# Attention and gated expert layer on one core: the masks built on DVE from index patterns instead of by GpSimd selections

## The chip, the cores and the metric

One Trainium2 chip, one core. The metric is the device time of one execution in microseconds, from the device's own clock; lower is better. Engines are named as in the profile: PE (TensorE's matrix multiplies), PEld (its weight loads), DVE (VectorE), ACT (ScalarE), POOL (GpSimd) and SP (the queue that issues the DMAs). Each engine takes its instructions strictly in program order and waits at the first one that isn't ready.

## What is computed

```python
B, H, S, D = 4, 8, 768, 64; block, window = 32, 16
k_sum = k.reshape(B, H, 24, 32, D).max(axis=3)
v_sum = v.reshape(B, H, 24, 32, D).mean(axis=3)
mask_l = np.abs(pos[:, None] - pos[None, :]) < window
scores_l = np.where(mask_l, scale * q @ k.T, -1e9)
scores_s = scale * q @ k_sum.T + np.log(32)
a = softmax(np.concatenate([scores_l, scores_s], -1))
attn = a @ np.concatenate([v, v_sum], axis=2)
x = attn.transpose(0, 2, 1, 3).reshape(B * S, H * D)      # 3072 x 512
out = ((x @ w_a) * (x @ w_b)) @ w_out                     # w: 512 x 1536, 512 x 1536, 1536 x 512
```

Each query sees the 31 keys nearest to it and 24 block summaries; then every row of 512 values goes through the gated layer. All is float32 at the edges; the matrix products run in a rounded 32-bit form with a high and a low part for each operand.

## The kernel before

**Tiles and stages.** The attention works on 128 queries at a time, in two halves of 64 (QT). A half needs a window of 96 keys (WIN) and the 24 summaries, so 120 score columns (COLS). The expert layer works on chunks of two or three such tiles; the list of (chunk, slice of the 1536 inner columns) is called items. The first two chunks (FILL = 2) go through eight of the twelve slices together as one wide item (PAIR), while the weights arrive from HBM and are converted (`convert`, lines 386 to 427: ACT L405, DVE L408 and L416, ACT L421, POOL L424, once for each of 36 weight parts). All later chunks use the converted weights. The head is what happens until the first items run: K tiles are loaded (L342) and turned on PE (L441), DVE takes block maxima (L508), ACT puts the keys into place (L500, L501), Q is turned and scaled (L938), masks are added on PE (L650), scores are made on PE (L663).

**The masks.** A tile `mask` of 128 partitions (query), 3 kinds (first tile of a sequence, inner tile, last tile) and 128 columns holds -1e9 where a key isn't seen, 0 where it is, and log 32 over the summaries. It is made on POOL (lines 214 to 237 and 322): one memset, then for each kind a row of `affine_select` (L229, 21 in all) and two small memsets (L234). Kinds 0 and 1 are made first, then POOL builds `pairs` (L241, L243), casts the identity (L317), splits the first two kinds into a high and a low part `maskr` (L318, L319), and makes kind 2 last. The first four tiles of attention add `maskr` on PE (L650); all later ones add `mask` on DVE (L692). DVE begins with three memsets (L252 twice for the value tiles `vbuf`, L253).

**The order of work.** Nothing is ordered by a compiler: every operation is handed to `Work.add` with an engine, a rank, an expected duration and the data that it reads and writes. `emit` then plays a simple clock: each engine takes the ready operation of the lowest rank, and the instructions are emitted in the order of that play. Two things steer it: `ORDER` (line 24), lists of operation numbers that fix the beginning of each engine's order, and `Work.free` (line 325), the time at which each engine is free when the play starts. When an engine's list is used up, the planner chooses by rank and by its own clock; past 70 us of that clock it adds a margin (SLACK) to what comes from another engine.

Of the kernel before, what the change touches and what calls it, by code (L numbers as in the profile page):

```python
# [10 lines left out]
F32R = mybir.dt.float32r  # L11
# [4 lines left out]
ALU = mybir.AluOpType  # L16
AX = mybir.AxisListType
LOG32 = 3.4657359027997265
NEG = -1.0e9
# [10 lines left out]
    ],  # L30
    "ACT": [
# [8 lines left out]
    ],  # L40
    "DVE": [
# [8 lines left out]
    ],  # L50
    "POOL": [
# [3 lines left out]
    ],  # L55
# [6 lines left out]
    ],  # L62
}

# [79 lines left out]
def attention_moe(  # L144
# [10 lines left out]
    nc = tc.nc  # L155
    B, H, S, D = q.shape
    P = 128
# [4 lines left out]
    QT = 64  # L162
    BLK = 32
    NS = S // BLK
    WIN = 96
    COLS = WIN + NS
    CH = 256
    G = CH // P
    WIDE = 3
# [17 lines left out]
    def sb(shape, name, dtype=F32):  # L187
        return const.tile(shape, dtype, tag=name, name=name)

    ident = sb([P, P], "ident")  # L190
    make_identity(nc, ident)

# [19 lines left out]
    kper = kT[:, :, : KC - 32].rearrange("p c (i x) -> p c i x", x=PER)  # L212

    mask = sb([P, 3, P], "mask")
    nc.gpsimd.memset(mask, 0.0)

    def mask_kind(i):
        for e in range(2):
            es = slice(e * QT, (e + 1) * QT)

            for c0, n, w in ((0, WIN, 0),) if e == 0 else ((0, 32, 0), (32 + NS, 64, 32)):
                sl = mask[es, i, c0 : c0 + n]
                bounds = [(1, w - 1, -1), (-1, 31 - w, 1)]
                if i == 0 and e == 0:
                    bounds.append((1, w - 16, 0))
                if i == 2 and e == 1:
                    bounds.append((-1, 79 - w, 0))
                for step, base, per_query in bounds:
                    nc.gpsimd.affine_select(  # L229
                        out=sl, in_=sl, compare_op=ALU.is_ge, fill=NEG, base=base,  # L230
                        pattern=[[step, n]], channel_multiplier=per_query,
                    )
            k0 = WIN if e == 0 else 32
            nc.gpsimd.memset(mask[es, i, k0 : k0 + NS], LOG32)  # L234

    mask_kind(0)
    mask_kind(1)


    pairs = sb([P, 96], "pairs")  # L240
    nc.gpsimd.memset(pairs, 1.0 / BLK)  # L241
    for base, sign in ((32, 1), (-31, -1)):
        nc.gpsimd.affine_select(  # L243
            out=pairs, in_=pairs, compare_op=ALU.is_ge, fill=0.0, base=base,
            pattern=[[-2 * sign, 96]], channel_multiplier=sign,
# [3 lines left out]
    pbuf = sb([P, 2, NP, P], "pt")  # L249
    vbuf = [sb([P, H, D], f"vw{e}") for e in range(2)]  # L250
    for e in range(2):
        nc.vector.memset(vbuf[e], 0.0)  # L252
    nc.vector.memset(sbuf[:, :, :, COLS:], 0.0)  # L253
    xt = sb([P, 9, NP, P], "x", F32R)
    last = xt[:, 0].rearrange("p c x -> p (c x)")
    gt, gg = sb([P, 2 * CH], "g"), sb([P, 2 * WIDE * P], "gh", F32R)
    ght, glt = gg[:, : WIDE * P], gg[:, WIDE * P :]
    gs = [gt[:, i * CH : (i + 1) * CH] for i in range(2)]
    ghs, gls = [ght[:, :CH], last[:, :CH]], [glt[:, :CH], last[:, CH:]]
# [1 line left out]
    half = sb([P, S // P, 8], "half")  # L261
# [46 lines left out]
    def area(i):  # L308
# [5 lines left out]
    maskr = [  # L314
        x[:, n : n + 2 * P].rearrange("p (i x) -> p i x", x=P) for n in (P, 3 * P)
    ]
    nc.gpsimd.tensor_copy(out=identr, in_=ident)  # L317
    nc.gpsimd.tensor_copy(out=maskr[0], in_=mask[:, :2, :])  # L318
    nc.gpsimd.tensor_tensor(  # L319
        out=maskr[1], in0=mask[:, :2, :], in1=maskr[0].bitcast(F32), op=ALU.subtract  # L320
    )
    mask_kind(2)


    work = Work({"POOL": 10.9, "DVE": 2.3, "ACT": 2.3, "PE": 3.0, "SP": 0.8})

    def pe(rank, takes, reads, writes, fn):
        work.add("PE", rank, takes, 0.25, reads, writes, fn)
# [949 lines left out]
```

## Time and profile before

| what | value |
|---|---|
| median of 3 runs | 654.04 us (653.34 to 654.15) |
| span of the profiled execution, first to last instruction | 652.4 us |
| own time of the profiled execution | not listed apart from the runs; its span is 1.6 us below their median |
| TensorE's mean granted clock | 0.997 of full speed |
| busy: PE, PEld, DVE, ACT, POOL | 639.0, 591.7, 398.0, 242.6, 155.8 us |

The page counts an engine as busy while one of its compute instructions is under way. A row of a timeline reads: start, duration, engine, source line, operation, output and input, shapes, how many in a row, and in brackets the idle time before it with what ended it. [...] A row of a group reads: line, engine, operation, shapes and count, then total busy us and mean ns of one, then idle time before the group and what ended it.

### The profile page before, as it was taken

The page shows a single profiled execution, that of the slowest core. Times are in us where ns is not written, and L with a number is a line of the kernel's source. Part 1 is how long each engine was busy: PE and PEld are TensorE (multiplying, and loading weights), DVE is VectorE, ACT ScalarE, POOL GpSimd, SP SyncE. Part 2 cuts the span into 40 slices and gives each one's busy share as a digit, 9 for nine tenths or more (in the row PEclk, how much of TensorE's full clock was granted, in tenths as well). Part 3 has the DMA queues.
Part 4 walks back from the last instruction along what each step waited for, and adds up shares of the span by engine and source line. Part 5 has one row for each costly group of instructions (what it writes and reads, how often), then busy time and mean ns, then how long its engine had stood idle before and what let it go on. Part 6 is the DMA issues. An engine that isn't in the chain of part 4 may idle for free.

```text
span 652.4 us, 12782 instructions
## 1 busy us (share of the span) xinstructions
PE 639.0 (98%) x4911; PEld 591.7 (91%) x4911; DVE 398.0 (61%) x866; ACT 242.6 (37%) x694; POOL 155.8 (24%) x238
## 2 busy tenths in 40 slices
PE   7799999999999999999999999999999999999997
PEld 4598888899999999999999999999999999999996
DVE  5877899987887584676676763756766632122212
ACT  4886787324443231422334312343323321121111
POOL 6782667523223222123222100111001100000000
PEclk9899999999999999999999999999999999999999
DMA  9999993552422233513114230142110200010001
GB/s 242 277 284 267 296 240 72 102 125 56 104 63 82 50 72 64 128 39 81 33 34 119 54 56 12 26 102 40 32 25 1 72 1 0 2 49 0 1 1 48
DMA packets 153108, 54.68 MB, mean 84 GB/s; under 512 B 133192, under 2 KB 145736, under 8 KB 153048
## 3 DMA queue, kind: packets, MB, share of 16 engines
q1 hardware_dynamic: 152904, 53.75, 34.0%
q8 instruction: 38, 0.62, 0.4%
q14 instruction: 22, 0.18, 0.1%
q10 hardware_dynamic: 144, 0.13, 0.1%
HBM read 47.12 MB, written 6.29 MB: 82 GB/s over the span
## 4 chain that ended last, share of the span: by engine, by line
PE 90%; DMA 4%; SPq 2%; ACT 1%; POOL 1%; DVE 1%; issue 0%; DVEq 0%; POOLq 0%; ACTq 0%
PE h L1067 55%; PE o L1154 28%; DMA raw<-in_moe_w_b_dram 4%; PE c L663 3%; PE o L816 3%; SPq L342 2%; POOL w L424 1%; PE h L816 0%; ACT S L405 0%; DVE c L408 0%; PE c L816 0%; PE c L1067 0%; POOL space L755 0%; DVE S L416 0%; PE o L768 0%
## 5 line engine op out<-in xcount | busy, mean ns | idle before, releaser
L1067 PE MATMUL h<-x,w 128*128 128x384 f32 (+2 forms) x2100 | 390.5, 320 | 0.1
L1067 PEld LDWEIGHTS h<-x,w 128*128 128x128 f32 x2100 | 334.1, 190 | 9.5 <-DVE x L839 0.7
L1154 PE MATMUL o<-w,gh 128*128 128x512 f32 x731 | 175.2, 382 | 0.0
L1154 PEld LDWEIGHTS o<-w,gh 128*128 128x128 f32 x731 | 134.5, 189 | 18.0 <-issue 2.4
L1135 DVE TENSOR_TENSOR h<-h,g 128x384 f32<-128x384 f32 (+1 forms) x79 | 45.7, 579 | 134.7 <-PE h L1067 134.3
L1137 ACT CAST gh<-h 128x384 fp32r<-128x384 f32 x71 | 34.0, 480 | 220.8 <-DVE h L1135 216.4
L800 DVE STREAM_TRANSPOSE pt<-s 32x256 f32<-32x256 f32 x228 | 99.3, 436 | 11.6 <-POOL s L755 7.9
L755 POOL TENSOR_TENSOR s<-s,nml 128x480 f32<-128x480 f32 x44 | 43.5, 989 | 229.6 <-DVE nml L751 193.6
L1067 PE MATMUL h<-late,w 128*128 128x384 f32 x288 | 94.0, 326 | 0.0
L729 ACT ACTIVATE s<-s,nml 128x120 f32<-128x120 f32 x160 | 61.5, 387 | 35.1 <-DVE nml L700 35.1
L1132 ACT COPY g<-h 128x384 f32<-128x384 f32 (+1 forms) x80 | 39.2, 490 | 55.4 <-PE h L1067 54.5
L1067 PEld LDWEIGHTS h<-late,w 128*128 128x128 f32 x288 | 54.4, 189 | 1.2 <-DVE late L839 0.2
L1140 DVE TENSOR_TENSOR gh<-h,gh 128x384 fp32r<-128x384 f32 x71 | 39.5, 556 | 22.0 <-ACT gh L1137 21.3
L692 DVE SCALAR_TENSOR_TENSOR s<-c,mask 128x480 f32<-128x480 f32 x40 | 26.0, 652 | 26.7 <-PE c L663 26.4
L587 POOL TENSOR_TENSOR S<-S 96x256 f32<-96x256 f32 (+3 forms) x58 | 33.2, 572 | 35.4 <-DMA S<-in_v_dram 32.9
L1154 PE MATMUL o<-w,x 128*128 128x512 f32 (+1 forms) x133 | 32.6, 381 | 0.2 <-DVE x L1108 0.2
L424 POOL TENSOR_TENSOR w<-S,w 128x512 fp32r<-128x512 f32 x24 | 30.4, 1286 | 7.3 <-ACT w L421 6.9
L408 DVE TENSOR_SCALAR c<-raw 128x512 int32<-128x512 uint32 x36 | 28.4, 804 | 5.6 <-DMA raw<-in_moe_w_b_dram 3.0
L729 ACT ACTIVATION_READ_ACCUMULATOR s<-s,nml 128x1 f32 x160 | 30.3, 190 | 0.0
L1154 PEld LDWEIGHTS o<-w,x 128*128 128x128 f32 x133 | 24.4, 189 | 4.2 <-DVE x L1108 0.6
L700 DVE TENSOR_REDUCE nml<-s 128x4 f32<-128x480 f32 x40 | 25.8, 647 | 0.5
L405 ACT ACTIVATE S<-raw 128x512 f32<-128x512 f32 x24 | 20.4, 861 | 4.7 <-DMA raw<-in_moe_w_b_dram 4.3
(138 smaller groups left out, 446.3 us busy)
## 6 DMA issues: line engine op xcount, KB each, us to landing
raw<-in_moe_w_a_dram SPq DMA_DIRECT2D x12, 512.0 KB, 7.7
raw<-in_moe_w_b_dram SPq DMA_DIRECT2D x12, 512.0 KB, 8.6
raw<-in_moe_w_out_dram SPq DMA_DIRECT2D x12, 512.0 KB, 5.7
out_dram<-S SPq DMA_DIRECT2D x23, 256.0 KB, 2.1
S<-in_v_dram SPq DMA_DIRECT2D x24, 192.0 KB, 2.8
kin<-in_k_dram SPq DMA_DIRECT2D x38, 100.0 KB, 2.5
qin<-in_q_dram SPq DMA_DIRECT2D x112, 32.0 KB, 1.9
vw<-in_v_dram SPq DMA_DIRECT2D x17, 192.0 KB, 2.8
```

The costliest lines, as they stand in the source:

```text
L408: dve(rank, 0.66, [raw], [bk], lambda: nc.vector.tensor_scalar(out=z.bitcast(I32), in0=word(0).bitcast(U32), scalar1=2.0**-29, scalar2=7.0 ...
L424: lambda eng=nc.vector if near else nc.gpsimd: eng.tensor_tensor(out=half(1), in0=t, in1=half(0).bitcast(F32), op=ALU.subtract),
L587: lambda: nc.gpsimd.tensor_tensor(out=out, in0=i0, in1=i1, op=ALU.add),
L729: lambda h=h, c=c, more=more: nc.scalar.activation(y[h][:, c, :], x[h][:, c, :], AF.Exp, bias=m[:, 0, h, c : c + 1], scale=1.0, **more,),
L755: lambda h=h, r=r: nc.gpsimd.tensor_tensor(out=y[h], in0=y[h], in1=r[:, :, None].broadcast_to([P, NP, COLS]), op=ALU.mult,),
L800: lambda js=js, qs=qs, rs=rs: nc.vector.transpose(out=pv[js, rs, qs], in_=sv[qs, rs, js]),
L1067: nc.tensor.matmul(ps, w[:, c, part, :], xs[xpart][:, :, c].rearrange("p g (a b) -> p g b a", a=2), start=(i == 0), stop=(i == n - 1),)
L1132: act(CHAIN, 0.13 + W / 1030, ["h0"], gk, lambda: nc.scalar.copy(out=g, in_=pa))
L1135: lambda: nc.vector.tensor_tensor(out=pb, in0=pb, in1=g, op=ALU.mult),
L1137: act(CHAIN, 0.16 + W / 1030, [bk], ghks, lambda: nc.scalar.copy(out=gh, in_=pb))
L1140: lambda: nc.vector.tensor_tensor(out=gl, in0=pb, in1=gh.bitcast(F32), op=ALU.subtract),
L1154: nc.tensor.matmul(b, (gh if first else gl)[:, j * P : (j + 1) * P], y, start=(f == 0 or half is not None) and first and part == 0, stop=( ...
```

## The change

Four edits:

1. POOL no longer makes masks. It writes, by three `iota`, a tile with key offset minus query index minus 16 (partition index with a factor of -1). The tile is `g`, which the items use much later as scratch.
2. DVE squares it, compares with 15.5 squared and multiplies the result by -1e9 for all three kinds at once, then patches with five memsets; the split into `maskr` moves from POOL to DVE too.
3. The two memsets of `vbuf` move from DVE to POOL, behind `pairs`.
4. `Work.free` says 5.0 for POOL (10.9 before) and 5.0 for DVE (2.3 before), and the end of each list in `ORDER` is cut off: 8 operations on PE, 22 on ACT, 24 on DVE, 8 on POOL, 7 on SP. What stays of the lists is unchanged.

```diff
@@ ORDER: the ends of the lists are cut
-        529, 530, 532, 321, 539, 537, 538, 540, 547, 545, 546, 548, 555, 553,
+        529, 530, 532, 321, 539, 537,
...
-        264, 276, 270, 310, 304, 316, 298, 363, 357, 375, 339, 387, 369, 381,
+        264, 276, 270, 310, 304, 316,
...
@@ behind make_identity
+    gt = sb([P, 2 * CH], "g")
+    steps, squares = gt[:, :COLS], gt[:, P : P + COLS]
+    for half, c0, n, w in ((0, 0, COLS, 0), (1, 0, 32 + NS, 0), (1, 32 + NS, 64, 32)):
+        nc.gpsimd.iota(
+            steps[half * QT : (half + 1) * QT, c0 : c0 + n], pattern=[[1, n]], base=w - BLK // 2,
+            channel_multiplier=-1, allow_small_or_imprecise_dtypes=True,
+        )
...
     mask = sb([P, 3, P], "mask")
-    nc.gpsimd.memset(mask, 0.0)
-    def mask_kind(i):
...
-    mask_kind(0)
-    mask_kind(1)
...
     for e in range(2):
-        nc.vector.memset(vbuf[e], 0.0)
+        nc.gpsimd.memset(vbuf[e], 0.0)
...
     nc.gpsimd.tensor_copy(out=identr, in_=ident)
-    nc.gpsimd.tensor_copy(out=maskr[0], in_=mask[:, :2, :])
-    nc.gpsimd.tensor_tensor(
+
+    nc.vector.tensor_tensor(out=squares, in0=steps, in1=steps, op=ALU.mult)
+    nc.vector.tensor_scalar(
+        out=mask[:, :, :COLS], in0=squares[:, None, :].broadcast_to([P, 3, COLS]),
+        scalar1=(BLK / 2 - 0.5) ** 2, scalar2=NEG, op0=ALU.is_gt, op1=ALU.mult,
+    )
+    nc.vector.memset(mask[:, :, COLS:], 0.0)
+    nc.vector.memset(mask[:QT, :, WIN:COLS], LOG32)
+    nc.vector.memset(mask[QT:, :, 32 : 32 + NS], LOG32)
+    nc.vector.memset(mask[:QT, 0, :16], NEG)
+    nc.vector.memset(mask[QT:, 2, COLS - 16 : COLS], NEG)
+    nc.vector.tensor_copy(out=maskr[0], in_=mask[:, :2, :])
+    nc.vector.tensor_tensor(
         out=maskr[1], in0=mask[:, :2, :], in1=maskr[0].bitcast(F32), op=ALU.subtract
     )
-    mask_kind(2)
...
-    work = Work({"POOL": 10.9, "DVE": 2.3, "ACT": 2.3, "PE": 3.0, "SP": 0.8})
+    work = Work({"POOL": 5.0, "DVE": 5.0, "ACT": 2.3, "PE": 3.0, "SP": 0.8})
```

## Rows read from the trace of the kernel before

**Rows 1.** The page: PE's share, and all engines.

```profile
PE 639.0 (98%) x4911; PEld 591.7 (91%) x4911; DVE 398.0 (61%) x866; ACT 242.6 (37%) x694; POOL 155.8 (24%) x238
```

**Rows 2.** Busy time by stretches: head, filling, full load, end.

```profile
0.00:24.00 24.00, 15.65 (x134) 11.14 (x135) 14.10 (x27) 12.60 (x38) 16.14 (x53) 0.95 1.06 263
24.00:60.00 36.00, 35.39 (x402) 31.44 (x401) 27.27 (x57) 28.25 (x65) 23.81 (x24) 0.98 1.01 262
60.00:640.00 580.00, 579.84 (x4334) 541.72 (x4333) 352.99 (x776) 198.66 (x586) 115.89 (x162) 1.00 0.28 66
640.00:652.40 12.40, 8.15 (x47) 7.42 (x45) 3.60 (x7) 3.09 (x6) 0.00 (x0) 1.00 0.17 63
```

**Rows 3.** Timeline of PE, first 20 us.

```profile
4.41 1.09 PE L441 MATMUL h<-ident,space 128*128 128x128 f32 x4 [4.41 <-POOL mask L229]
...
10.29 1.11 PE L441 MATMUL o<-ident,space 128*128 128x128 f32 x4
...
11.90 1.17 PE L650 MATMUL o<-space 128*128 128x512 f32 x4
12.99 1.05 PE L663 MATMUL o<-kT,qT 64*64 64x120 f32 x32
...
19.02 0.65 PE L768 MATMUL o<-ident,s 128*120 128x128 f32 x4 [2.49 <-POOL s L755]
```

**Rows 4.** Timeline of POOL, first 10 us.

```profile
1.09 0.29 POOL masks.py:199 TENSOR_SCALAR_AFFINE_SELECT ident<-ident 128x128 f32<-128x128 f32 x1
...
6.16 0.60 POOL L243 TENSOR_SCALAR_AFFINE_SELECT pairs<-pairs 128x96 f32<-128x96 f32 x2
6.71 0.29 POOL L317 CAST space<-ident 128x128 fp32r<-128x128 f32 x1
...
7.44 0.72 POOL L319 TENSOR_TENSOR space<-mask,space 128x256 fp32r<-128x256 f32 x1
```

**Rows 5.** Groups by line, first 12 us: what is removed or moved.

```profile
L229 POOL TENSOR_SCALAR_AFFINE_SELECT mask<-mask 64x96 f32<-64x96 f32 (+2 forms) x21 | 4.8, 238 | 1.1
...
L252 DVE MEMSET vw<- 128x512 f32 x2 | 1.0, 485 | 1.0 <-PEq L1258 1.0
...
L253 DVE MEMSET s<- 128x64 f32 x1 | 0.1, 112 | 0.0
```

**Rows 6.** Timelines of DVE and ACT in the head, from 5 us.

```profile
5.53 0.69 DVE L508 TENSOR_REDUCE ksum<-h 128x16 f32<-128x512 f32 x1 [3.44 <-PE h L441]
...
7.83 0.43 ACT L500 COPY kT<-c 128x320 f32<-128x320 f32 x1 [0.37 <-PE c L441]
...
11.44 0.69 DVE L508 TENSOR_REDUCE ksum<-o 128x16 f32<-128x512 f32 x1 [0.45 <-PE o L441]
12.17 0.26 DVE L522 COPY kT<-ksum 128x192 f32<-128x192 f32 x1
```

**Rows 7.** Groups by line and shape, whole span: nearest operations to the added ones.

```profile
L1135 DVE TENSOR_TENSOR h<-h,g 128x384 f32<-128x384 f32 x71 | 40.2, 566 | 132.0 <-PE h L1067 131.6
...
L1103 DVE TENSOR_TENSOR h<-h,g 128x256 f32<-128x256 f32 x20 | 8.6, 430 | 10.7 <-ACT g L1100 10.5
...
L570 DVE TENSOR_TENSOR ksum<-half 128x23 f32<-128x23 f32 x12 | 2.6, 218 | 0.0
...
L424 POOL TENSOR_TENSOR w<-S,w 128x512 fp32r<-128x512 f32 x24 | 30.4, 1286 | 7.3 <-ACT w L421 6.9 <-POOL w L424 0.2
...
L1033 POOL MEMSET S<- 128x1024 f32 x1 | 1.0, 964 | 0.0
```

**Rows 8.** Busy time by stretches: the dip of the clock; the stretch newly planned.

```profile
21.00:26.00 5.00, 4.28 (x28) 3.21 (x31) 3.06 (x9) 3.71 (x7) 2.04 (x5) 0.66 1.07 235
81.00:113.00 32.00, 32.00 (x176) 27.73 (x176) 30.41 (x52) 26.37 (x53) 23.35 (x20) 1.00 0.65 155
```

**Rows 9.** Timelines of DVE and PEld where the third chunk begins.

```profile
137.35 0.68 DVE L839 TENSOR_TENSOR x<-c,x 128x512 fp32r<-128x512 f32 x1
...
138.08 2.08 PEld L1067 LDWEIGHTS h<-x,w 128*128 128x128 f32 x18 [0.27 <-DVE x L839]
```

More of the change, by code (lines that the diff above doesn't have):

```diff
@@ L214, in attention_moe @@
     mask = sb([P, 3, P], "mask")
-    nc.gpsimd.memset(mask, 0.0)
-    def mask_kind(i):
[L218 to L234, printed above, removed]
-    mask_kind(0)
-    mask_kind(1)
     pairs = sb([P, 96], "pairs")
@@ L255, in attention_moe @@
     last = xt[:, 0].rearrange("p c x -> p (c x)")
-    gt, gg = sb([P, 2 * CH], "g"), sb([P, 2 * WIDE * P], "gh", F32R)
+    gg = sb([P, 2 * WIDE * P], "gh", F32R)
     ght, glt = gg[:, : WIDE * P], gg[:, WIDE * P :]
```

9 rows, old and new, of the table ORDER are left out of this document.

## The prediction

> **What bounds the kernel now.** I read the page first: PE is busy 98% of the span [rows 1]. Then the busy time by stretches [rows 2], because an average over the span hides where the missing 2% are. From 60 to 640 us PE lacks 0.16 of 580 us, and from 24 to 60 us it lacks 0.61 of 36. What is left is 8.35 us of idle time before 24 us and 4.25 us in the last 12 us, where the last outputs are added, copied and stored. So only two kinds of change can move the end: PE's work starting earlier in the first 24 us, or PE being made to wait later, where it now doesn't. Third, the timeline of PE in the head [rows 3]. The first transposes of K start at 4.41 us and the sixth set at 10.29, that is 1.18 us apart, which is longer than a set takes (1.09); the sets come as fast as the K tiles arrive by DMA. The trace puts the first wait, 4.41 us, down to a mask selection on POOL. I don't take that as the cause: these transposes read the identity and a K tile; the identity was ready at 1.09 + 0.29 = 1.38 us [rows 4], and the K tiles' own spacing counted back from the later sets gives the same start. Masks enter PE at 11.90 us [rows 3]; POOL had finished their split at 7.44 + 0.72 = 8.16 us [rows 4], 3.7 us sooner. Masks therefore wait for PE, not PE for masks.
>
> **The change, part by part.**
>
> *POOL's selections go.* 21 selections of 0.238 us, 4.8 us of work [rows 5], and the split with them. All of it lies beside DMA-paced transposes, and its product has 3.7 us to spare. Worth: 0. What hides it is the arrival of K; without that cover masks would be needed when Q is turned, still not at 1.38 us.
>
> *Three iotas come.* No row shows an iota. The nearest is the selection, which writes an index-driven pattern over the same 64 partitions: 0.238 us [rows 5]. The lower bound is a short memset's 0.112 [rows 5], the upper one the longest POOL operation on one tile, 1.286 us for 128x512 with two inputs [rows 7]. I take 0.24, since shape and kind are nearest. They follow the identity, so they end at 1.38 + 3 x 0.24 = 2.1 us, and between 1.7 and 5.2 us at the bounds.
>
> *DVE makes the masks.* This is an added wait: DVE's queue is in order, the squares wait for POOL, and behind them stands all of DVE's head, with ACT's key copies and PE's scores behind that. The square of 128x120 lies between 0.218 (23 columns) and 0.430 (256 columns) [rows 7]; I take 0.32. The compare writes 360 columns: 0.57, after 384 columns in 0.566. Its bounds are 0.43 and 0.69, by the 256-column product [rows 7] and the reduction of 512 columns [rows 6]. Five memsets at 0.112 [rows 5] make 0.56. Copy and subtraction over 256 columns are 0.43 each [rows 7], 0.86; for the copy alone 0.26 [rows 6] is the low end. Sum 2.3 us, so DVE is done at 4.4 us, bounds 3.6 and 7.8. The two value memsets of 0.485 leave DVE [rows 5], but they lay ahead of everything and give nothing back.
>
> What DVE owes first is the reduction at 5.53 us [rows 6], for which it idled 3.44 us. Lateness there is first eaten by gaps: 0.37 us before ACT's copy at 7.83, 0.45 us before the reduction at 11.44, and, because the summaries are in place at 12.17 + 0.26 = 12.43 us and the scores start at 12.99 [rows 3], 0.56 us more. That is 1.38 us, so PE's scores move only if DVE's masks end after 6.9 us. At 4.4 us they don't. `maskr` is needed at 11.90. Worth: 0.
>
> [...]
>
> If DVE has to stand back for POOL, for whatever reason, the price goes by rows: POOL's pairs (0.60), identity cast (0.29) [rows 4] and the two value memsets (0.96 together, by 128x1024 in 0.964 [rows 7]) are 1.9 us, so DVE ends at 6.3 instead of 4.4. Still below 6.9: 0 again, unless the iotas are slow too.
>
> *Value memsets on POOL.* 0.96 us; their readers are DMA loads that SP issues far behind the head, and POOL, even so, has 4.8 - 0.7 - 0.96 = 3.1 us less to do than before. SP's queue passes nothing new: no DMA is moved within the kept lists.
>
> *The planner.* `Work.free` can't reorder the head, because the lists fix it. The cut frees the order from about 81 us on, where PE has its wide items. PE's sum of work is the same in any order, and the margin there is in DVE: 30.41 of 32 us busy from 81 to 113 us, ACT 26.37, POOL 23.35, PE without a gap [rows 8]. Behind the lists' old end the planner chose alone, and PE has no gap worth naming until 640 us [rows 2]. Expected 0; below 0 by at most the 0.16 us of gaps [rows 2]; above 0 by what the second rival costs.
>
> *Sum:* 652.4 + 0 = 652.4 us of span. The median of the runs shown is 1.6 us above that span, so 654.0.
>
> **The rivals.**
>
> *A: faster, because the clock no longer dips.* [...] It fell after PE had been held up, the longest time 2.49 us before 19.02 us [rows 3]. [...] For it: another rhythm of POOL and DVE in the head. Against it: that wait is for POOL's softmax product, whose place in the order is kept.
>
> *B: slower, because the replanned stretch delays the third chunk.* The third chunk's second attention tile is made on DVE, ACT and POOL beside the weight conversions. Its low part is written from 137.35 to 138.03 us, and PE's weight load of the chunk's first item waits 0.27 us for it [rows 9]. So there is no reserve: any lateness of that chain is PE's. If the planner puts two conversions on POOL (1.286 each [rows 7]) ahead of that chain, PE waits 2.6 us: 656.6. PE loses from the first lateness on; past 1.3 us it can be measured. For it: DVE's fullness [rows 8]. Against it: the planner has margins there, and its rank puts attention behind conversions in both kernels.
>
> *C: slower, because DVE's masks come late.* With iotas at 1.286 us DVE ends at 7.8 by its own work and at up to 9.7 if POOL holds it up too. It decides at 6.9 us, and costs PE 0.9 to 2.8 us, 1.9 in the middle: 655.9. [...] For it: iota is unseen here. Against it: it needs three iotas each five times as long as a selection.
>
> *D: the change does not do what it says,* since the kept lists end where the planner would choose the same: no change either, and part of the forecast.
>
> **How the numbers follow.** What a measurement of this kernel can tell from no change is about 0.2%, 1.3 us. No change has 0.72, with its own range 653.2 to 654.9 (the runs' spread and small gaps). A has 0.08 (652.3), B 0.14 (656.6), C 0.06 (655.9). Only A is faster by over 1.3 us; B and C are slower. The range goes from 652.9 to 656.6: A stays out, and a part of B.
>
> **What would show it.** Right: PE's first transposes still at 4.4 us, masks on PE at 11.9, scores at 13.0; DVE's subtraction for `maskr` done before 5.5 us; POOL idle from about 5 to 12 us; PE without gaps from 60 to 640 us. Wrong: first transposes well before 4.4 us (then the masks did pace PE); scores after 13.0 (C); an idle PE near 138 us (B); a granted clock of 1.00 from 21 to 26 us (A).

## The result and the profile after

The changed kernel takes 661.37 us (median of 4 runs, 661.12 to 661.64) against 654.10 us before in the same session (4 runs, 653.34 to 655.2): ratio 1.0113, 95% interval 1.0099 to 1.0127. It is 7.3 us slower. The forecast of 654.0 us is wrong, and the time lies above the range too. The profiled execution took 661.4 us with a span of 659.4, 2.0 us more than its span. Lines of the changed kernel behind the masks are 13 lower than before (PE's L1067 is L1054, DVE's L1135 is L1122).

The page's shares first, then busy time by stretches, both of the kernel after. A row by stretches, here as in [rows 2] and [rows 8], has the stretch, its length, then for PE, PEld, DVE, ACT and POOL the busy time with the number of instructions, then the clock granted to TensorE as a share of its full speed, the share of the DMA engines and GB/s:

```profile
PE 640.2 (97%) x4911; PEld 591.5 (90%) x4911; DVE 402.1 (61%) x873; ACT 243.0 (37%) x694; POOL 150.5 (23%) x213
```

```profile
0.00:24.00 24.00, 14.64 (x136) 10.49 (x136) 15.92 (x35) 13.88 (x40) 11.11 (x28) 0.94 1.08 264
24.00:60.00 36.00, 35.27 (x402) 31.59 (x401) 27.58 (x57) 28.10 (x65) 24.28 (x24) 0.99 1.06 274
60.00:640.00 580.00, 575.10 (x4292) 535.21 (x4291) 353.91 (x774) 197.41 (x585) 115.09 (x162) 1.00 0.28 65
...
82.00:110.00 28.00, 25.70 (x139) 21.60 (x138) 26.57 (x45) 22.82 (x45) 21.22 (x18) 0.94 0.59 139
110.00:260.00 150.00, 149.00 (x1253) 137.27 (x1252) 113.19 (x266) 49.24 (x174) 42.48 (x73) 1.00 0.36 79
260.00:285.00 25.00, 23.40 (x183) 21.44 (x182) 12.90 (x34) 8.51 (x27) 5.57 (x11) 1.00 0.44 100
```

POOL has lost 5.3 us of work and DVE gained 4.1, as the change says. The loss is in the third row: PE, without a gap before [rows 2], lacks 4.9 us from 60 to 640 us. It lies in three places: 2.30 us before 110, 1.00 up to 260, 1.60 around 270. In the first of them the mean granted clock is 0.94, which is another 28 x 0.06 = 1.7 us of PE's work lost: the granted clock is 0.50 from 89.56 to 92.97 us, with PE busy all of these 3.41 us, just behind the longest wait, and 1.00 on both sides, so this comes on top of the idle time. Together that is 6.6 us; the head gives about 0.5 back (the first wide item of 12 matrix products starts at 60.61 us, 61.09 before), and the spans differ by 7.0. So 0.9 us aren't placed by these rows.

The waits of PE in that stretch (what waited, for whom; us in total, times, longest), and PE's timeline at the longest (it had run the second half of a slice up to 86.56 us):

```profile
PE o L1141 <- ACT x L1124: 2.3, 1, 2.3
PE o L1141 <- ACT gh L1124: 1.2, 1, 1.2
PE h L1054 <- DVE x L826: 1.0, 2, 0.7
PE h L1054 <- DVE late L826: 0.3, 1, 0.3
```

```profile
83.81 2.75 PE L1054 MATMUL h<-x,w 128*128 128x512 f32 x12
88.85 3.13 PE L1141 MATMUL o<-w,x 128*128 128x512 f32 x8 [2.30 <-ACT x L1124]
```

PE's down product at 88.85 us waits for ACT's cast of the gated product, ACT for DVE's product, and DVE's timeline shows where that one stands:

```profile
85.99 0.79 DVE L395 TENSOR_SCALAR c<-raw 128x512 int32<-128x512 uint32 x1
86.88 0.69 DVE L403 SCALAR_TENSOR_TENSOR S<-S,c 128x512 int32<-128x512 int32 x1
87.49 0.69 DVE L1122 TENSOR_TENSOR h<-h,g 128x512 f32<-128x512 f32 x1
```

Behind a row of weight conversions (L395, L403): its input was there at 86.56 us, so the conversions hold it up by 0.9 us. The rest of the 2.3 us is the product and the cast themselves (87.49 to 88.80 us), which nothing in PE's order covers. The head, by contrast, went as forecast. POOL, DVE and PE there:

```profile
1.33 0.57 POOL L190 IOTA g<- 64x120 f32 x3
...
2.94 0.98 POOL L229 MEMSET vw<- 128x512 f32 x2
3.88 0.34 POOL L294 CAST space<-ident 128x128 fp32r<-128x128 f32 x1
```

```profile
1.94 0.28 DVE L296 TENSOR_TENSOR g<-g 128x120 f32<-128x120 f32 x1 [0.94 <-POOL g L190]
2.25 0.41 DVE L297 TENSOR_SCALAR mask<-g 128x360 f32<-128x360 f32 x1
...
3.30 0.77 DVE L306 CAST space<-mask 128x256 fp32r<-128x256 f32 x1
4.10 0.42 DVE L307 TENSOR_TENSOR space<-mask,space 128x256 fp32r<-128x256 f32 x1
5.42 0.69 DVE L495 TENSOR_REDUCE ksum<-h 128x16 f32<-128x512 f32 x1 [0.89 <-PE h L428]
```

```profile
4.30 1.08 PE L428 MATMUL h<-ident,space 128*128 128x128 f32 x4 [4.30 <-POOL space L294]
...
11.81 1.17 PE L637 MATMUL o<-space 128*128 128x512 f32 x4
12.91 1.05 PE L650 MATMUL o<-kT,qT 64*64 64x120 f32 x32
```

These answer to [rows 3], [rows 4] and [rows 6]: first transposes at 4.30 us (4.41), masks on PE at 11.81 (11.90), scores at 12.91 (12.99), DVE's masks done at 4.10 + 0.42 = 4.52.

### The profile page after: what moved, and what is told of

It is laid out like the page before. It is cut to its first block, busy times and chain, and to the rows that moved or that the text cites. A ratio compares the mean times of both kernels' runs of the same rounds, so it can differ in the third digit from the quotient of the medians.

```text
span 659.4 us, 12751 instructions
## 1 busy us (share of the span) xinstructions
PE 640.2 (97%) x4911; PEld 591.5 (90%) x4911; DVE 402.1 (61%) x873; ACT 243.0 (37%) x694; POOL 150.5 (23%) x213
## 4 chain that ended last, share of the span: by engine, by line
PE 81%; DVE 8%; SPq 3%; DMA 3%; POOL 1%; issue 1%; ACT 1%; DVEq 0%; POOLq 0%; ACTq 0%
PE h L1054 50%; PE o L1141 25%; SPq L329 3%; PE o L803 3%; PE c L650 3%; DVE pt L787 2%; DMA raw<-in_moe_w_b_dram 1%; DMA space<-in_v_dram 1%; DVE c L395 1%; DVE S L787 1%; POOL space L897 1%; DVE S L403 1%; DMA S<-vm 1%; POOL s L742 1%; DVE h L1090 1%
## 5 line engine op out<-in xcount | busy, mean ns | idle before, releaser
L1054 PE MATMUL h<-x,w 128*128 128x384 f32 (+2 forms) x2100 | 391.0, 320 | 1.1 <-DVE x L826 1.0
L1054 PEld LDWEIGHTS h<-x,w 128*128 128x128 f32 x2100 | 334.2, 190 | 11.0 <-DVE x L826 1.7
L1122 DVE TENSOR_TENSOR h<-h,g 128x384 f32<-128x384 f32 (+1 forms) x79 | 45.8, 580 | 132.6 <-PE h L1054 132.2
L1054 PE MATMUL h<-late,w 128*128 128x384 f32 x288 | 94.0, 326 | 0.3 <-DVE late L826 0.3
L1054 PEld LDWEIGHTS h<-late,w 128*128 128x128 f32 x288 | 54.4, 189 | 1.6 <-DVE late L826 0.6
L395 DVE TENSOR_SCALAR c<-raw 128x512 int32<-128x512 uint32 x36 | 28.0, 792 | 3.5 <-DMA raw<-in_moe_w_b_dram 1.7
L803 PEld LDWEIGHTS o<-pt,vw 120*64 120x64 f32 x576 | 18.3, 138 | 4.9 <-issue 4.1
```

The source lines that it names most:

```text
L395: dve(rank, 0.66, [raw], [bk], lambda: nc.vector.tensor_scalar(out=z.bitcast(I32), in0=word(0).bitcast(U32), scalar1=2.0**-29, scalar2=7.0 ...
L803: nc.tensor.matmul(ps[h * D : (h + 1) * D, c, es], vw[e][:COLS, 2 * c + h, :], d[:COLS, h, c, es], start=True, stop=True, tile_position=(0 ...
L1054: nc.tensor.matmul(ps, w[:, c, part, :], xs[xpart][:, :, c].rearrange("p g (a b) -> p g b a", a=2), start=(i == 0), stop=(i == n - 1),)
L1122: lambda: nc.vector.tensor_tensor(out=pb, in0=pb, in1=g, op=ALU.mult),
```

## The experiments

Numbers such as 540 are the planner's operation numbers in `ORDER`. Around the end of the lists: 540 on PE is the second half of the wide item's sixth slice, 547 the first half of the next; 542 is DVE's product of that slice, 543 ACT's cast of it, 544 DVE's difference for its low part.

### 1 and 2: the two halves of the change apart

```diff
 run 1: masks as after, ORDER as before
 run 2: masks as before; in ORDER, on all five engines:
-        ..., 321, 539, 537, 538, 540, 547, 545, 546, 548, 555, 553,
+        ..., 321, 539, 537,
```

> The masks on DVE and the value memsets on POOL as in the change, with the uncut lists of the kernel before. Theory 1 (all of the loss is in the order of work that the cut left to the planner; the masks cost nothing): 653.0 to 654.5 us, ratio to before 0.998 to 1.001, PE without gaps from 60 to 640 us; the head's 0.9 us lead of the changed kernel at 65 us (64.50 against 65.40) may stay. Rival (DVE's masks cost time): 658 us or more.

> The kernel before with nothing changed but the ends of the lists cut; masks by POOL's selections, the planner's free times as before. Theory 1: all of the loss, 660.5 to 662.5 us, with PE idle near 87 us for 2 us or more. Rival (the masks cost time): 653.5 to 655 us.

Measured: the masks alone 653.57 us (11 runs), ratio 0.9999 [0.9991, 1.0008]; the cut alone 661.50 us (4 runs), ratio 1.0121 [1.0106, 1.0137]. The masks cost nothing; the shortened lists cost all of it. By the planner's play run 1 has the order of the kernel before and run 2 that of the kernel after, on all five engines, so the new `Work.free` alone changes no order. Busy time by stretches and DVE's timeline, masks alone:

```profile
82.00:110.00 28.00, 28.00 (x141) 24.29 (x143) 26.52 (x45) 24.63 (x49) 21.14 (x19) 1.00 0.69 163
110.00:260.00 150.00, 150.00 (x1294) 139.43 (x1283) 112.79 (x275) 49.63 (x175) 43.69 (x74) 1.00 0.37 81
260.00:285.00 25.00, 25.00 (x194) 23.58 (x193) 16.87 (x39) 8.47 (x27) 5.52 (x10) 1.00 0.35 91
```

```profile
82.91 0.69 DVE L408 SCALAR_TENSOR_TENSOR S<-S,c 128x512 int32<-128x512 int32 x1
83.90 0.70 DVE L1127 TENSOR_TENSOR h<-h,g 128x512 f32<-128x512 f32 x1 [0.30 <-PE h L1059]
```

DVE is just as full (26.52 of 28 us against 26.57), so it isn't that DVE has more to do: with the full lists the product stands at 83.90, 3.6 us earlier, because there PE runs 540, which it needs, ahead of 547; and it waits for PE, not PE for it.

The planner's own clock (the play in `emit`, not a measurement) says how the cut starts it. Behind 538 it stands at 82.08 us on PE; 540 is ready for it at 82.35, and it considers only what is ready within 0.15 us. So it takes 547, where the list named 540. In runs 1 and 2 theory 1 was the shortened lists as a whole; from here on it is that near-tie, and the next runs try it.

### 3: that swap alone

```diff
 order of the kernel after written out as lists, and on PE:
-        538, 547, 545, 540,
+        538, 540, 547, 545,
```

> The changed kernel with its own order of all engines written out to 140 us of the planner's clock, and two neighbours on PE swapped: the second half of slice 5 (operation 540) before the first half of slice 6 (547). DVE's order is unchanged, so the product (542) still stands behind the conversion step 385. Theory 1a (the gap needs DVE's place too): DVE reaches 542 at about 87.5 us as before, PE runs out of work at the same time, 660 to 662 us. Rival 1b (PE's order alone is the loss): the 2.3 us gap and the clock dip behind it go, 657 to 658 us.

Measured: 661.42 us, ratio 1.0118 [1.0104, 1.0132]; the wait of 2.3 us stays. PE's place alone does nothing as long as DVE and ACT come to the slice as late as they do.

### 4: two more entries, planner free behind them

```diff
-        ..., 321, 539, 537,
+        ..., 321, 539, 537, 538, 540,
```

> The changed kernel with two more entries in PE's list (538, 540), which make the planner wait for 540 instead of taking 547; all behind it is planned by the planner on that basis, with 542 three places earlier on DVE. Theory 1a: the gap of 2.3 us at 88 us and the half clock behind it (1.7 us) go: 656.5 to 658 us, and what is left above 654 is the planner's order later on. Rival (the stretch is too full on DVE for any plan but the list): 660 us or more.

Measured: 657.70 us, ratio 1.0063 [1.0049, 1.0077]. As theory 1a expected, about half comes back. The planner goes another way on all engines; the first gap is gone, the one near 270 us stays (1.2 us in the waits), and 0.5 us at 95 us is new.

### 5: the planner told longer conversions

```diff
-        act(CHAIN, 0.68, [raw], [room], ...
+        act(CHAIN, 0.80, [raw], [room], ...
-        dve(rank, 0.66, [raw], [bk], ...
+        dve(rank, 0.74, [raw], [bk], ...
-            rank, 0.6, [room, bk], [raw, key],
+            rank, 0.61, [room, bk], [raw, key],
```

> The changed kernel with the planner's expected durations of three conversion steps raised towards the trace's (L392 0.68 to 0.80, L395 0.66 to 0.74, L403 0.60 to 0.61 us), lists cut as in the change. Rival 2 (the planner's clock runs ahead of DVE and ACT, and so it places the products too late): 655 to 658 us. Theory 1 (one near decision on PE, which these durations don't turn: the planner still takes 547 ahead of 540): 660 to 662.5 us, the gap at 88 us stays.

Measured: 659.39 us, ratio 1.0079 [1.0064, 1.0095]. That lies between the two ranges, under theory 1's 660 and above rival 2's 658, so it settles neither. The wait near 89 us is 1.5 us, the one near 270 gone, and 0.6 to 0.7 us each stand at 195, 199 and 200 us instead. Longer durations take back 2 of the 7.3 us, through another order with gaps of its own; that the durations are the cause isn't shown.

### 6 and 7: three places by hand; a wider window

```diff
 run 6: as run 3, and on DVE and ACT:
-        372, 373, 378, 379, 384, 385, 542, 390, 391, 544,
+        372, 373, 542, 378, 379, 384, 385, 390, 391, 544,
-        377, 374, 383, 380, 389, 395, 543, 549,
+        377, 374, 543, 383, 380, 389, 395, 549,
 run 7: kernel after, in emit:
-                (o for o in choices(engine) if o.est <= now + 0.15),
+                (o for o in choices(engine) if o.est <= now + 0.30),
```

> The changed kernel's order written out to 140 us of the planner's clock, with three operations moved: on PE 540 ahead of 547, on DVE the product 542 four conversion steps earlier (ahead of 378), on ACT the cast 543 ahead of 383. Nothing else differs. Theory 1a (the gap is these three places together): the 2.3 us gap at 88 us and the half clock behind it go, 656.5 to 658.5 us. Rival (replanning behind them was what helped in the run with two more entries): 660 us or more.

> The changed kernel with the planner's window widened from 0.15 to 0.30 us: an operation may be chosen if it is ready within that time. At the cut 540 is ready 0.27 us after PE is free by the planner's clock, so the wider window takes it and the narrow one takes 547. All later decisions may turn too. Theory 1: the gap at 88 us goes; 653.5 to 658 us, the spread because later decisions are open. Rival: 660 us or more.

Measured: 661.42 us (1.0112 [1.0095, 1.0129]) and 661.46 us (1.0112 [1.0097, 1.0127]). In both theory 1 misses and the time lies in the rival's range, 660 us or more. The wait at 88 us is gone in both, so the reason given for it holds, and in both the time is the same as without, so theory 1 falls: the near-tie places the first gap, it doesn't set the loss. What helped run 4 was then the new order behind its two entries, as run 6's rival has it, and not these places. In run 6 the wait moves to the next operand on the same chain; in run 7 it breaks into seven kinds of 0.2 to 1.2 us. The waits of PE in run 6 and the first of run 7:

```profile
PE o L1155 <- DVE gh L1141: 2.0, 1, 2.0
PE o L1155 <- ACT gh L1138: 1.2, 1, 1.2
PE h L1068 <- DVE x L840: 1.0, 2, 0.7
```

```profile
PE o L1141 <- ACT gh L1124: 1.2, 1, 1.2
PE h L1054 <- DVE x L826: 1.0, 1, 1.0
PE o L1141 <- ACT x L1124: 0.9, 1, 0.9
```

### 8 and 11: how late may DVE's masks be?

```diff
 masks as after, ORDER as before, and
+    for _ in range(21):          # 9 in run 11
         nc.vector.tensor_tensor(out=squares, in0=steps, in1=steps, op=ALU.mult)
```

> The masks on DVE with the uncut lists, and 20 more squares of 128x120 ahead of the masks (0.28 us each by the changed kernel's trace, 5.6 us in all), so that DVE's masks end at about 10 us instead of 4.5. By the prediction's slack DVE's masks may end at 6.9 us; past that PE's scores move one to one: scores at about 16 us instead of 12.9, 656 to 657 us. Rival (the weights' arrival by DMA absorbs it): 653.5 to 654.5 us with scores late all the same.

> As the run with 20 more squares, with 8: 0.31 us each there, 2.5 us in all, so DVE's masks end at about 6.6 us (the copy's 0.77 us beside POOL's work shrinks to 0.29). The prediction's slack says that they may end at 6.9 us without cost: 653.2 to 654.2 us, scores at 12.9 to 13.1 us. Rival (each us of DVE's lateness counts from the first): 655 us or more.

Measured: 657.27 us (1.0048 [1.0032, 1.0063]) and 653.60 us (0.9992 [0.9982, 1.0002]). The ends of the masks on DVE, run 8 and then run 11:

```profile
9.64 0.29 DVE L312 CAST space<-mask 128x256 fp32r<-128x256 f32 x1
9.97 0.43 DVE L313 TENSOR_TENSOR space<-mask,space 128x256 fp32r<-128x256 f32 x1
```

```profile
5.84 0.29 DVE L312 CAST space<-mask 128x256 fp32r<-128x256 f32 x1
6.17 0.42 DVE L313 TENSOR_TENSOR space<-mask,space 128x256 fp32r<-128x256 f32 x1
```

Masks that end at 6.17 + 0.42 = 6.59 us are free. Masks that end at 10.40 cost 657.27 - 654.09 = 3.2 us against the kernel before in the same session (2.1 to 4.1 by the interval). If each microsecond then costs one, which isn't shown, the cost begins at 10.40 - 3.2 = 7.2 us, between 6.3 and 8.3. Forecast: 6.9. PE's scores start at 16.93 us in run 8 (about 16 expected) and at 13.64 in run 11 (12.9 to 13.1 expected); in run 1 it was 14.01, at no cost, so the start of the scores alone is no measure of it.

### 9 and 10: a fourth place, and the keys near 270 us

```diff
 run 9: as run 6, and on DVE:
-        384, 385, 390, 391, 544,
+        384, 544, 385, 390, 391,
 run 10: as run 9, order written out to 300 us; DVE: 1235 to 1237 ahead of 1176,
         PE: 1305 ahead of 1179, as the kernel before has them
```

> As the run with three places, and a fourth: on DVE the difference 544 ahead of the conversion step 385. With three places the first down product had its operand in time and the second one waited 2.0 us for 544 instead. Theory 1b (a chain of two products and two casts per item, each of which has to stand early enough in its own engine's queue): the gap near 90 us goes, 657 to 658.5 us, as with the two entries that let the planner do the same. Rival (something else in the stretch holds PE up by the same 2 us): 660 us or more.

> As the run with four places, order written out to 300 us, and at the end of a later chunk, near 270 us, the last three steps of the key preparation (1235 to 1237) ahead of the product 1176 on DVE and the next tile's products and scores (1305) ahead of the down product 1179 on PE, as the kernel before has them. Theory 1c (what the two entries left, 4 us, lies half in this one place: PE idle 1.24 and 0.36 us there): 1.5 to 2.1 us less than the run with four places, 655 to 657 us. Rival (the rest lies elsewhere): the same as the run with four places.

Measured: 661.62 us (1.0120 [1.0103, 1.0137]) and 659.86 us (1.0091 [1.0076, 1.0106]). Run 9 misses: the wait moves on by one more item, and grows. PE's timeline and its stretch in run 9:

```profile
89.05 5.34 PE L1068 MATMUL h<-x,w 128*128 128x512 f32 x24
97.30 2.91 PE L1155 MATMUL o<-w,x 128*128 128x512 f32 x8 [2.91 <-ACT x L1138]
```

```profile
90.00:105.00 15.00, 12.09 (x49) 9.98 (x48) 13.91 (x22) 11.84 (x20) 11.32 (x10) 0.89 0.46 114
```

Run 10 misses in its absolute time, which built on run 9, but its step is right: 1.76 us less than run 9 (1.5 to 2.1 expected), and the 1.60 us of gaps from 260 to 285 us are gone:

```profile
260.00:285.00 25.00, 25.00 (x194) 23.58 (x193) 14.88 (x37) 8.38 (x27) 6.92 (x13) 1.00 0.44 100
```

The place near 270 us is a cost of its own. There, too, a down product waits for ACT's cast of the gated product (1.24 us in the kernel after, at 273.25).

### 12 to 15: the full lists, shortened one engine after another

```diff
 masks as after; the list's end cut off as in the change (-) or kept (+):
 run 12: + PE  + ACT  + DVE  + POOL  - SP
 run 13: + PE  + ACT  + DVE  - POOL  - SP
 run 14: + PE  - ACT  + DVE  - POOL  - SP
 run 15: + PE  + ACT  - DVE  - POOL  - SP
```

> The change with the full lists on PE, ACT, DVE and POOL, and SP's alone shortened: the order on the four computing engines is then the one of the kernel before, and only SP starts some loads in another order. Theory 2 (the order of the computing engines carries the loss): 653 to 654.3 us. Rival (the loads of the weights come late for the conversions, and their order carries it): 656 us or more.

> SP's and POOL's lists shortened, the other three full. Theory 2a (PE, DVE and ACT carry it; POOL's few conversion halves have room): 653 to 655 us. Rival 2b (POOL's order is at fault, since the half of a conversion that PE's item waited for in the planner stands on POOL): 657 us or more.

> Lists full on PE and DVE alone. Theory 2c (the products stand too late in DVE's queue, so DVE's order with PE's is enough): 655 us or less. Rival 2d (ACT's order of its halves of the conversions, on which each DVE step waits, is needed as well): 656.5 to 661.5 us.

> Lists full on PE and ACT alone. Theory 2c: DVE's order is free again, so much of the loss comes back, 656.5 to 661.5 us. Rival 2d: 655 us or less. Both this run and the one with PE and DVE over 656.5 us: it takes the two together.

| run | us | ratio |
|---|---|---|
| 12, SP cut | 653.96 | 1.0005 [0.9995, 1.0015] |
| 13, SP and POOL cut | 653.88 | 0.9995 [0.9986, 1.0004] |
| 14, ACT cut too | 660.49 | 1.0098 [1.0083, 1.0113] |
| 15, DVE cut instead of ACT | 665.33 | 1.0167 [1.0149, 1.0186] |

SP's and POOL's ends are worth nothing. Take away either ACT's 22 entries or DVE's 24 and the loss is back. Run 14 is in rival 2d's range and not in 2c's; run 15 is above both, 2c's 656.5 to 661.5 us and 2d's 655 or less, and what was written for both runs above 656.5 us holds: it takes the two together. PE's 8 entries were kept in all four runs. By the planner's play, cutting PE's list as well would change run 13's order in one place only, 547 ahead of 540 on PE; that order wasn't run, so whether DVE's and ACT's entries are enough without PE's isn't shown. The waits of PE from 60 to 640 us, all of run 14 and the first of run 15; in run 13 there are none:

```profile
PE o L804 <- DVE pt L788: 2.0, 1, 2.0
PE h L1055 <- ACT x L823: 0.7, 1, 0.7
PE h L1055 <- DVE late L827: 0.4, 1, 0.4
```

```profile
PE o L804 <- DVE pt L788: 3.2, 2, 3.0
PE o L1142 <- ACT gh L1125: 1.2, 1, 1.2
```

Run 14 has no wait at all in the stretch where its list differs; it pays at 195 to 198 us, where PE waits for the last of twelve transposes of an attention tile on DVE. They end at 195.09 us, in run 13 at 190.64. So the order that was taken early still counts 100 us later. In the kernel after the difference shows earlier, in DVE's groups between 60 and 112 us. Masks alone, and then the kernel after:

```profile
L792 DVE STREAM_TRANSPOSE pt<-s 32x256 f32<-32x256 f32 x7 | 3.0, 433 | 0.1
```

```profile
L787 DVE STREAM_TRANSPOSE pt<-s 32x256 f32<-32x256 f32 x3 | 1.3, 431 | 0.0
...
L536 DVE STREAM_TRANSPOSE kT<-kin 128x576 f32<-128x576 f32 x1 | 0.8, 778 | 0.0
```

Left to itself, the planner there does keys of a later chunk early (none of these key rows stands in that stretch with the full lists, where the first is at 117.40 us) and transposes of the present attention late: 3 instead of 7. This doesn't explain run 14: its first key row is at 118.23 us, and it has 5 transposes in that stretch, as many as run 13, which loses nothing. So no one early sign of the loss, common to these orders, is shown.

## Why the prediction was wrong

**The step that failed** is the planner's: "Expected 0 … above 0 by what the second rival costs". It argued that PE's sum of work is the same in any order and that behind the lists' old end the planner, alone, left no gap worth naming [rows 2]. Both hold, and neither carries the conclusion. That the planner kept PE fed from the lists' old end on was shown for the state in which those lists left it. Without the lists' ends it starts from another state, in a stretch where DVE is busy 30.41 of 32 us [rows 8], and PE has gaps from there up to 285 us. The entries that the runs show to count are DVE's 24 and ACT's 22. The term put at 0 measured +7.3 us (661.37 against 654.10; run 2: +7.8), of which the rows of the kernel after show 4.9 as waits and 1.7 as clock.

**Rival B** had the kind right, not the place or size. It named a replanned stretch, DVE's fullness, and an attention chain late for the third chunk. That wait is there, 0.65 us at 142.10 us for DVE's L826, the same low part as in [rows 9]; but it is a tenth of the loss. The larger waits are those of down products for the gated product (2.3 us at 89 us, 1.2 at 273), and what the runs show behind them is DVE's and ACT's order, not two conversions on POOL: run 13 cuts POOL's list at no cost.

**POOL's selections**, worth 0: right (run 1). **The iotas**: 0.57 us for three, 0.19 each against 0.24; done at 1.90 us, 2.1 forecast. **DVE's masks**: done at 4.52 us, 4.4 forecast. Singly the terms were further off: square 0.28 (0.32), compare 0.41 (0.57, below its lower bound of 0.43), memsets 0.46 in all (0.56), copy 0.77 (0.43), subtraction 0.42 (0.43). That the sum came out right is partly luck: 0.34 us too little for the copy against 0.31 too much for the rest. The compare was probably too dear because a one-input operation was priced by rows with two inputs: in runs 8 and 11 the copy, with one input, takes 0.29 us, the subtraction, with two, 0.42 to 0.43 over the same 256 columns. **POOL's saving** was put at 3.1 us and was 5.3: the sum left out the split and the mask's memsets, which went too. **The slack to 6.9 us**: in keeping with runs 8 and 11, which set it between 6.59 and 10.40 us.

**The copy** shows the one place in DVE's masks where DVE and POOL seem to have stood in each other's way. It took 0.77 us while POOL filled the value tiles (2.94 to 3.92 us) and cast the identity (3.88 to 4.22), and 0.29 in run 8, where POOL idled from 4.28 to 15.96 us, and in run 11: 0.48 us. The compare ran beside POOL's short memsets and selections without such a loss: 0.41 us at 2.25 us in the kernel after, 0.41 at 8.59 us in run 8 with POOL idle. The square took 0.28 us beside a memset; in run 8, most of the time without POOL, 21 of them took 6.62 us, 0.32 each.

A standstill for all of POOL's 1.9 us, which would have put DVE's end at 6.3, didn't come: DVE's masks ended at 4.52 us. What held the copy up beside POOL isn't shown.

**Rival A**: no run shows the 1.7 us that its 652.3 takes off the span; the granted clock from 21 to 26 us is 0.66 as before [rows 8]. **C** needed slow iotas and falls. **D** falls: the kept lists don't end where the planner would choose the same.

**What stays open.** Why several quite different orders (the cut, three places, four places, the wider window) end within 0.3 us of each other at 661.5 isn't shown; I know of no bound that would make them, and it may be chance. Nor is any single entry shown to carry the loss: runs 14 and 15 say that it takes DVE's and ACT's together.

## What to carry to other kernels

An order that is written out by hand up to some point also fixes the state from which a planner goes on; shortening it is a change to everything behind it, even where the planner alone looked flawless before. Price it by the slack of the in-order queues there (in run 8 DVE's first reduction, whose input PE had done at 4.20 + 1.09 = 5.29 us, stood behind the masks until 10.31): here DVE was busy 95% of a stretch in which PE had nothing in reserve. And when a moved gap doesn't change the time, stop moving it: take the lists away one engine at a time instead. Four such runs told which engines' entries count; the orders by hand hadn't.

## What was not expected of the hardware

Where PE waited, it lost more than the length of its waits. In run 14 PE is idle 3.15 us between 193 and 198.4 us, and from 190 to 210 us the granted clock is 0.78 and 0.88, between the two values that it had in the kernel after (0.50 from 89.56 to 92.97 us, 1.00 before and behind):

```profile
190.00:200.00 10.00, 6.76 (x49) 4.93 (x49) 8.20 (x18) 4.58 (x19) 0.42 (x1) 0.78 0.43 121
200.00:210.00 10.00, 10.00 (x53) 9.76 (x52) 5.86 (x14) 1.68 (x5) 3.68 (x7) 0.88 0.09 25
```

That is 10 x 0.22 + 10 x 0.12 = 3.4 us at full speed. Part of it falls on idle time. If the clock was at 0.50 here too, it was so for 2.2 / 0.5 = 4.4 us before 200 us and 1.2 / 0.5 = 2.4 us behind, about 195.6 to 202.4 us; by PE's timeline PE is busy 5.7 us of that, so by this estimate 2.9 us of PE's work are lost beside the idle time itself. It doesn't follow from the wait's length alone: the profile of the cut alone (run 2) has the same 2.3 us of waiting at 89 us as the kernel after and a granted clock of 1.00 there, where the kernel after has 0.94 from 82 to 110 us:

```profile
82.00:110.00 28.00, 25.11 (x141) 21.07 (x140) 26.99 (x44) 22.90 (x45) 21.19 (x18) 1.00 0.60 138
```

That profiled execution took 660.22 us, 1.3 us less than run 2's median. What decides between the two isn't shown.
